# A pause of the attention filled, its second q in two pieces, pooling shared, and the steps ahead of a loop reordered

## The chip, the cores and the metric

The kernel runs on one core of a Trainium2 chip. The metric is the time of one execution on the device in microseconds (us), lower is better. Times stand in the text as the profile gives them: PE is the engine of the matrix products (TensorE), PEld its loads of the stationary operand, DVE is VectorE, ACT is ScalarE, POOL is GpSimd, and SP is SyncE, which here only issues DMAs.

## What is computed

Three stages, in fp32 throughout (cut from the reference):

```python
# attention over pooled keys: q, k, v of shape (8, 8, 576, 64), every 8 rows of k and v averaged
k_p = k.reshape(B, H, 72, 8, D).mean(axis=3)
v_p = v.reshape(B, H, 72, 8, D).mean(axis=3)
attn = softmax(matmul(q, k_p.T) / sqrt(D))
x = matmul(attn, v_p)                       # 4608 rows of 512
# first mixture: rows with x @ w_skip > 0 go through their best of 8 experts
e_idx = argmax(xc @ w_gate); gate_w = softmax(xc @ w_gate)[e_idx]
x[do] = xc + gate_w * (relu(xc @ w1[e]) @ w2[e])
# second stage, for all rows
h = x @ w_in
out = (h / (1 + exp(-h))) @ w_out
```

## The kernel before

**Three stages in time.** The attention takes up to about 147 us, the expert stage from there to about 463 us (a first unit of up to 384 rows until 183 us, the rest in a loop that is entered at 184 us), the dense stage the rest. The change touches the attention's beginning and the step between the first unit and the loop. Every operation is issued through a wrapper that keeps the program's order on its engine (`Ordered`), so all rows of the profile carry line 117, that of its call, and the order in the text of the program is the order in each engine's queue. DMAs on a queue go in the order in which they are issued.

**The attention** (`attention`, line 180) treats 36 tiles of 128 rows, nine for a pair of batches of 576 rows: tiles 0 to 3 are the first 512 rows of batch 0, tiles 4 to 7 those of batch 1, and tile 8 is the last 64 rows of both. Tile 4 is thus the first that needs anything of batch 1. For each tile the steps are: `products` (line 291), eight matmuls of q with the pooled keys in block form (kbd) into PSUM tiles named s; `scores` (line 303), on DVE two maxima (mx) and on ACT eight exponentials (prb); `ptrans` (line 316), five transposes on PE (pt) and two copies on ACT (pts); `pv` (line 326), ten matmuls with the values (vex); and `post` (line 336) on DVE, which begins with sm and divides the row (x). The values of a batch also carry nine columns for routing: `router1` (line 257) transposes the pooled values (vtp, three matmuls), copies them on ACT (vt) and multiplies them with the router's weights wr (cps; the first batch's PSUM tile is named router), and `router2` (line 272) puts the result into vex. A batch is read by SP in three loads: k and v and q, 1152 KB each (`loadk`, `loadv`, `loadq`, lines 203 to 214). `pool_k` (line 216) sums eight rows of k, on DVE as one reduction for each half or quarter of k (kp), on POOL as three adds of halving length; `pool_v` (line 229) does the same for v in five chunks of 128 columns each, as reductions on DVE or adds on POOL; `keys` (line 252) writes kbd on ACT, `values` (line 245) writes vex on POOL.

The start (lines 367 to 388) issues 18 matmuls on a tile of ones (`WARM`, line 54; named warm in the trace), loads half of k0 twice, the constants, q0's first 128 columns, v0 in two pieces, q0's second 128 columns, q0's last 320 columns, wr (72 KB) and k1. The loop over tiles (line 393) runs from -2; its pass i does the scores of tile i+2 up to i = 3 and of i+3 behind it, the transposes of tile i+1, pv and post of tile i. Pass -2 loads v1 and q1 in one piece each, behind k1. DVE pools one half of k1 in pass -1 and the other in pass 0, POOL pools all of v1 in pass -1, and `router1(1)` comes at the end of pass 2. Which pass takes the four quarters of a later batch's k stands in a table (`KEYS`, line 43); that of batch 2 is `(2, 3, 4, 4)`. Batch 2's k and v are issued at the end of pass -2, behind q1.

**The step before the loop** (`first_unit`, line 995, in `moe`, line 852). Products of the unit with w2 of its expert: `mm2_two` (line 938) does sub-tiles 2 and 1, `mm2(0)` (line 926) sub-tile 0, 24 matmuls in eight groups of three (f = 0 to 7), between which steps can be put. Beside them:

- `ffn_ops(0)` (line 1182): four passes of DVE over 128x1024 elements that prepare the dense stage's weights (raw, raw, fr, fr in the trace), all four ahead of `mm2_two`; `ffn_conv3(0)` (line 1198) then casts them on ACT (fh) and subtracts on POOL (fl); `ffn_load(3)` (line 1165) is a load by SP into fr, which can start when fl is done;
- `xtrans` (line 684): transposes of the next unit's gathered rows (xn) on PE (xtp), a cast on ACT (xth) and a subtraction on DVE (xtl), for four chunks of 128 columns, in the order in which the loop's first matmuls (hp) read them;
- two `post` (DVE, x), a scatter (POOL), and small index operations (gi, si).

The loop's first pass then loads the next w1 (SP), does `post(0)`, gathers the rows of the unit after (POOL, xn<-xa), and runs `mm1`: hp (12 matmuls for each of eight f), hh and w2h on ACT. The placing before:

```python
for _ in self.ffn_ops(0):        # all four
    pass
self.rows(gi, nxt)
two = mm2_two()
...
mm2(0, gt, {2: ends, 6: lambda: self.xtrans((2, 3))})
```

Of the kernel before, what the change touches and what calls it, by code (L numbers as in the profile page):

```python
# [5 lines left out]
F32 = mybir.dt.float32  # L6
# [12 lines left out]
P = 128  # L19
# [22 lines left out]
EARLY = 18  # L42
KEYS = {2: (2, 3, 4, 4), 3: (6, 6, 7, 8), 4: (11, 12, 13, 13), 5: (15, 15, 16, 17), 6: (20, 20, 21, 22),
        7: (24, 24, 25, 26)}
# [8 lines left out]
ROWS = WB11, WT[0], WT[1], WB22, WT[2], WB21, WT[3]  # L53
WARM = 18
OPS = [2, 2, 2, 0, 4, 4]
# [104 lines left out]
class Kern:  # L160
# [19 lines left out]
    def attention(self, xa, rs, extra):  # L180
# [3 lines left out]
        with tc.tile_pool(name="as", bufs=1) as s1, \  # L184
# [26 lines left out]

            def loadq(b):
                q_t[b] = s2.tile([P, 4, S], F32, name=f"q{b}", tag="q", bufs=3)
                nc.sync.dma_start(q_t[b], self.qT[b])

            def pool_k(b, eng, halves=(0, 2), n=2):
                k = k_t[b]
                kp = st.get((b, "k"))
                if kp is None:
                    kp = st[b, "k"] = s2.tile([P, 4, G], F32, name=f"kp_{b}", tag="kp")  # L220
                if eng is nc.vector:
                    for a in halves:
                        eng.tensor_reduce(kp[:, a:a + n], k[:, a:a + n], AX.X, ALU.add)
                else:
                    eng.tensor_tensor(k[:, :, :, 0:4], k[:, :, :, 0:4], k[:, :, :, 4:8], ALU.add)
                    eng.tensor_tensor(k[:, :, :, 0:2], k[:, :, :, 0:2], k[:, :, :, 2:4], ALU.add)
                    eng.tensor_tensor(kp, k[:, :, :, 0], k[:, :, :, 1], ALU.add)

# [137 lines left out]
            nc.vector.memset(one, 0.0)  # L366
            self.warm(pp.tile([P, 1024], F32, name="warm", tag="pv"), WARM)
            k_t[0] = s2.tile([P, 4, G, POOL], F32, name="k0", tag="k")
# [3 lines left out]
            nc.scalar.dma_start(self.ident, self.con[:, 0:P])  # L372
            q_t[0] = s2.tile([P, 4, S], F32, name="q0", tag="q", bufs=3)
            nc.sync.dma_start(q_t[0][:, :, 0:P], self.qT[0][:, :, 0:P])
            nc.scalar.activation(one, one, AF.Exp)
            loadv(0)
            nc.sync.dma_start(q_t[0][:, :, P:2 * P], self.qT[0][:, :, P:2 * P])
            nc.sync.dma_start(q_t[0][:, :, 2 * P:S], self.qT[0][:, :, 2 * P:S])
            nc.sync.dma_start(wr, self.wr)
            loadk(1)  # L380
            for i in range(NB):
# [11 lines left out]
            for i in range(-2, NTILE):  # L393
                n = 3 if i > DEEP else 2
                if i > 0 and i + n < NTILE:
                    pss = products(i + n)
                    pts[i + 1] = ptrans(i + 1, prs.pop(i + 1))
                    prs[i + n] = scores(i + n, pss)
                elif i != -1 and i <= DEEP:
                    prs[i + 2] = scores(i + 2)  # L400
                if len(self.to_place) > (3 if i < EARLY else 0) and i < NTILE - 1:
                    self.place(1, nc.scalar.last)
                extra(i, True)
                ready = todo.pop(0) if todo and i < NTILE - 1 else None
                if ready and ready[0]:
                    ready[0]()
                if i == -2:
                    pool_v(0, on_dve=slice(0, 2), rest=slice(2, 3))
                    pool_v(0, on_dve=slice(4, 5), rest=slice(3, 4))
                    values(0)  # L410
                    loadv(1)
                    loadq(1)
                if i == -1:
# [6 lines left out]
                if i == -1:  # L420
                    prs[1] = scores(1, pss)
                    router2(0)
                    pool_k(1, nc.vector, (0,))
                    pool_v(1)
                    values(1)
                if i > 0:
# [20 lines left out]
                if i == 0:  # L447
                    pool_k(1, nc.vector, (2,))
                    keys(1)
                for b in range(B):  # L450
# [4 lines left out]
                    if i + 2 == first[b]:  # L455
                        if b + 2 < B:
                            loadk(b + 2)
                            loadv(b + 2)
                    if i + 2 == first[b] + 3 + (b == 0) and b + 1 < B:
                        router1(b + 1)  # L460
# [391 lines left out]
    def moe(self, xa, up):  # L852
        nc, tc, c = self.nc, self.tc, self.c
        with tc.tile_pool(name="ms", bufs=1) as s1, \
# [140 lines left out]
            def first_unit(cols, nxt):  # L995
                gates()
                nc.vector.tensor_scalar(self.s2, cols[:, U - 1:U], -1.0, None, ALU.add)
                self.ffn_abs(0, self.raw1[:, 0], self.raw1[:, 1])
                for _ in self.ffn_ops(0):
                    pass  # L1000
                self.rows(gi, nxt)
                two = mm2_two()

                def ends():
                    self.xtrans((0, 1))
                    for s in (2, 1):
                        o = self.x4[:, U if s == 2 else s]
                        post(s, two[s], gt, o)
                        if s == 2:
                            scatter(s, o=o)  # L1010
                            nc.vector.tensor_scalar(si[:, 0:U - 1], cols[:, 0:U - 1], -1.0, None, ALU.add)
                    self.ffn_conv3(0)
                    self.ffn_load(3)
                mm2(0, gt, {2: ends, 6: lambda: self.xtrans((2, 3))})

# [967 lines left out]
```

## Time and profile before

| | |
|---|---|
| median of 3 runs | 1229.18 us (1227.0 to 1232.85) |
| the profiled execution | 1231.53 us |
| its span in the profile | 1229.8 us |
| mean granted clock of TensorE | 0.996 of full speed |

All times inside the kernel come from the one profiled execution; its span is 1.73 us shorter than its own time. A timeline's row gives the start and the duration of a run of equal operations in us, the tiles written and read, the shape and their count, and in brackets the idle time of the engine just before with what ended it. "issue" there means that the engine waited for nothing that the profile shows. The clock is granted at one of two levels, 2.4 GHz (1.00 in the rows) or 1.2 GHz (0.50).

### The profile page before, as it was taken

What the parts mean: (1) busy time and instruction counts of PE and PEld (TensorE: products, weight loads), DVE (VectorE), ACT (ScalarE), POOL (GpSimd) and SP (SyncE); (2) the same over time, 40 slices, a digit from 0 to 9 for tenths busy, and PEclk for the clock granted to TensorE, in tenths of its full rate; (3) what the DMA queues carried; (4) which work ended last, traced back from release to release, by engine and by line L of the source; (5) the groups of instructions that cost most, each with busy time, mean ns of one, the idle gap of its engine ahead of it and who ended that gap; (6) DMA issues with size and microseconds to landing.
All of it is one profiled execution on the core that took longest, in us unless ns stands there. A gap on an engine that the chain in (4) does not pass through costs nothing.

```text
span 1229.8 us, 20291 instructions
## 1 busy us (share of the span) xinstructions
PE 1197.8 (97%) x6191; PEld 1014.5 (82%) x6192; DVE 930.5 (76%) x1574; ACT 616.9 (50%) x1290; POOL 395.3 (32%) x347
## 2 busy tenths in 40 slices
PE   8999898999999999999999999999999999999997
PEld 6988788998888888888888888888878888888885
DVE  6888886666776769988678855677897778977767
ACT  6877544445565445454444435554455544555441
POOL 5477532222231220423366823122211221112220
PEclk9999999999999999999999999999999999999999
DMA  9998547565575734558758783677657786575645
GB/s 374 336 305 273 174 138 267 156 213 182 186 252 193 229 139 104 170 165 270 236 180 294 237 248 106 222 202 200 220 187 240 218 232 219 185 245 184 195 159 146
DMA packets 162768, 260.70 MB, mean 212 GB/s; under 512 B 41669, under 2 KB 91461, under 8 KB 160000
## 3 DMA queue, kind: packets, MB, share of 16 engines
q1 hardware_dynamic: 150880, 241.39, 61.2%
q0 software_dynamic: 7008, 16.80, 4.4%
q10 hardware_dynamic: 4800, 1.51, 0.5%
q8 instruction: 42, 0.69, 0.2%
q14 instruction: 38, 0.31, 0.1%
HBM read 203.16 MB, written 59.18 MB: 213 GB/s over the span
## 4 chain that ended last, share of the span: by engine, by line
PE 56%; DVE 2%; DMA 2%; issue 1%; ACT 0%; POOL 0%; POOLq 0%; DVEq 0%
PE ps L117 18%; PE fopy L117 16%; PE fop L117 11%; PE fh L117 11%; DMA wout<-wdo 2%; PE yp L117 1%; PE yz L117 0%; DVE fr L117 0%; DVE accc L117 0%; DVE raw L117 0%; DVE c L117 0%; ACT c L117 0%; DMA out<-oc 0%; DVE w2l L117 0%; PE hp L117 0%
## 5 line engine op out<-in xcount | busy, mean ns | idle before, releaser
L117 PE MATMUL fopy<-c,wout 128*128 128x512 f32 x810 | 192.5, 391 | 1.5 <-DMA wout<-wdo 1.4
L117 PEld LDWEIGHTS fopy<-c,wout 128*128 128x128 f32 x810 | 150.8, 188 | 36.9 <-DVE accc L117 2.6
L117 POOL TENSOR_TENSOR tm<-tm,tm 128x512 f32<-128x512 f32 x24 | 31.8, 1323 | 271.2 <-ACT tm L117 271.2
L117 DVE TENSOR_TENSOR accc<-fopy,accc 128x1024 f32<-128x1024 f32 (+1 forms) x73 | 87.8, 1204 | 22.9 <-PE fopy L117 22.8
L117 ACT ACTIVATE hh<-hp 128x256 fp32r<-128x256 f32 (+1 forms) x96 | 39.5, 411 | 112.1 <-PE hp L117 107.5
L117 DVE TENSOR_TENSOR w2l<-raw,w2h 128x512 fp32r<-128x512 f32 x96 | 65.8, 690 | 27.5 <-ACT w2h L117 20.4
L117 ACT CAST c<-hs 128x512 fp32r<-128x512 f32 x96 | 59.7, 622 | 52.6 <-DVE hs L117 25.9
L117 ACT COPY tm<-ps 128x512 f32<-128x512 f32 x72 | 42.0, 583 | 84.4 <-PE ps L117 84.4
L117 DVE TENSOR_TENSOR c<-hs,c 128x512 fp32r<-128x512 f32 x96 | 66.0, 687 | 23.6 <-ACT c L117 23.6
L117 POOL TENSOR_TENSOR sw<-sw 128x256 f32<-128x256 f32 x64 | 72.4, 1154 | 35.5 <-DVE sw L117 34.2
L117 PE MATMUL fh<-w1l,fh 128*128 128x512 f32 x336 | 83.0, 389 | 0.0
L117 PE MATMUL hp<-xth,w1h 128*128 128x256 f32 (+2 forms) x384 | 72.7, 311 | 7.7 <-issue 3.1
L117 ACT ACTIVATE fsg<-fh 128x512 f32<-128x512 f32 x48 | 28.7, 597 | 91.4 <-PE fh L117 86.9
L117 PEld LDWEIGHTS fh<-w1l,fh 128*128 128x128 f32 x336 | 63.1, 188 | 13.1
L117 POOL DMA_INDIRECT xn<-xa,gi x33 | 38.5, 1165 | 109.4 <-PE hp L117 89.3
L117 PE MATMUL hp<-xth,w1l 128*128 128x256 f32 (+2 forms) x384 | 70.8, 306 | 0.0
L117 PE MATMUL hp<-xtl,w1h 128*128 128x256 f32 (+2 forms) x384 | 70.3, 305 | 0.0
L117 DVE TENSOR_TENSOR fgl<-fsg,fgh 128x512 fp32r<-128x512 f32 x48 | 39.1, 815 | 40.3 <-ACT fgh L117 40.3
L117 PEld LDWEIGHTS hp<-xth,w1h 128*128 128x128 f32 x384 | 59.6, 189 | 12.1 <-issue 6.6
L117 ACT ACTIVATE prb<-s,mx 128x72 f32<-128x72 f32 x288 | 65.4, 355 | 5.8 <-DVE mx L117 5.8
L117 PE MATMUL fop<-fl,fgh 128*128 128x512 f32 x168 | 65.4, 389 | 0.0
L117 PE MATMUL fop<-fh,fgh 128*128 128x512 f32 x168 | 65.4, 389 | 0.0
(260 smaller groups left out, 3025.2 us busy)
## 6 DMA issues: line engine op xcount, KB each, us to landing
raw<-w SPq DMA_DIRECT2D x88, 512.0 KB, 4.8
wout<-wdo SPq DMA_DIRECT2D x135, 256.0 KB
win<-wdi SPq DMA_DIRECT2D x36, 512.0 KB
w1l<-wdi SPq DMA_DIRECT2D x36, 512.0 KB
xa<-x SPq DMA_DIRECT2D x36, 256.0 KB
v<-vR SPq DMA_DIRECT2D x7, 1280.0 KB
w1l<-wdo SPq DMA_DIRECT2D x33, 256.0 KB
fr<-w_in SPq DMA_DIRECT2D x16, 512.0 KB
```

The costliest lines, as they stand in the source:

```text
L117: ins = f(*a, **k)
```

## The change

In the attention: four more matmuls on ones at the start and ten more in pass -2, behind tile 0's scores; wr is issued ahead of q0's last piece; q1 is issued in two pieces, the first 64 columns ahead of v1 and the other 512 behind it. One half of k1 is pooled by POOL in pass -1, ahead of v1; the other stays with DVE in pass 0, and keys(1) is split likewise. Of v1 POOL pools chunks 0 to 2, DVE chunks 3 and 4 in pass 2, behind the maxima of tile 4; values(1) follows there. k2's first quarter moves from pass 2 to pass 3, router1(1) from the end of pass 2 to pass 3, behind scores(5) and ahead of pv(3). In `first_unit`: three of the four operations of `ffn_ops(0)` stay ahead of `mm2_two`; the fourth and gi go behind the transposes of chunks 0 and 1 (still at f = 2); the transposes of chunks 2 and 3 go from f = 6 to f = 4, and the two posts, the scatter, si, the cast and the load go behind them.

```diff
-KEYS = {2: (2, 3, 4, 4), ...
+KEYS = {2: (3, 3, 4, 4), ...
-WARM = 18
+WARM, KEEP = 22, 10
...
-            def loadq(b):
-                q_t[b] = s2.tile([P, 4, S], F32, name=f"q{b}", tag="q", bufs=3)
-                nc.sync.dma_start(q_t[b], self.qT[b])
+            def loadq(b, *parts):
+                if b not in q_t:
+                    q_t[b] = s2.tile([P, 4, S], F32, name=f"q{b}", tag="q", bufs=3)
+                for c in parts or (slice(S),):
+                    nc.sync.dma_start(q_t[b][:, :, c], self.qT[b][:, :, c])
...
                 else:
-                    eng.tensor_tensor(k[:, :, :, 0:4], k[:, :, :, 0:4], k[:, :, :, 4:8], ALU.add)
-                    eng.tensor_tensor(k[:, :, :, 0:2], k[:, :, :, 0:2], k[:, :, :, 2:4], ALU.add)
-                    eng.tensor_tensor(kp, k[:, :, :, 0], k[:, :, :, 1], ALU.add)
+                    for a in halves:
+                        x = k[:, a:a + n]
+                        eng.tensor_tensor(x[:, :, :, 0:4], x[:, :, :, 0:4], x[:, :, :, 4:8], ALU.add)
+                        eng.tensor_tensor(x[:, :, :, 0:2], x[:, :, :, 0:2], x[:, :, :, 2:4], ALU.add)
+                        eng.tensor_tensor(kp[:, a:a + n], x[:, :, :, 0], x[:, :, :, 1], ALU.add)
...
-            nc.sync.dma_start(q_t[0][:, :, 2 * P:S], self.qT[0][:, :, 2 * P:S])
             nc.sync.dma_start(wr, self.wr)
+            loadq(0, slice(2 * P, S))
             loadk(1)
...
+                if i == 2:
+                    pool_v(1, (), slice(3, NC))
+                    values(1)
+                if i == 0:
+                    pool_k(1, nc.vector, (0,))
+                    keys(1, slice(0, 2))
...
                 if i == -2:
+                    self.warm(ones, KEEP)
...
+                    loadq(1, slice(P // 2))
                     loadv(1)
-                    loadq(1)
+                    loadq(1, slice(P // 2, S))
...
-                    pool_k(1, nc.vector, (0,))
-                    pool_v(1)
-                    values(1)
+                    pool_k(1, nc.gpsimd, (2,))
+                    pool_v(1, rest=slice(0, 3))
+                if i == 3:
+                    router1(1)
                 if i > 0:
                     pv(i, pts.pop(i))
...
                 if i == 0:
-                    pool_k(1, nc.vector, (2,))
-                    keys(1)
+                    keys(1, slice(2, 4))
...
-                    if i + 2 == first[b] + 3 + (b == 0) and b + 1 < B:
+                    if i + 2 == first[b] + 3 and 0 < b < B - 1:
                         router1(b + 1)
...
-                for _ in self.ffn_ops(0):
-                    pass
-                self.rows(gi, nxt)
+                ops = self.ffn_ops(0)
+                for _ in range(3):
+                    next(ops)
                 two = mm2_two()
                 def ends():
                     self.xtrans((0, 1))
+                    next(ops)
+                    self.rows(gi, nxt)
+                def sums():
+                    self.xtrans((2, 3))
                     for s in (2, 1):
...
-                mm2(0, gt, {2: ends, 6: lambda: self.xtrans((2, 3))})
+                mm2(0, gt, {2: ends, 4: sums})
```

## Rows read from the trace of the kernel before

**Rows 1.** The page, part 1: busy time, share and instructions of each engine
```profile
PE 1197.8 (97%) x6191; PEld 1014.5 (82%) x6192; DVE 930.5 (76%) x1574; ACT 616.9 (50%) x1290; POOL 395.3 (32%) x347
```

**Rows 2.** Busy time by stretch: stretch, us, PE, PEld, DVE, ACT, POOL, clock, DMA, GB/s
```profile
12.00:15.00 3.00, 3.00 (x15) 2.97 (x15) 1.35 (x3) 0.51 (x2) 2.50 (x7) 0.50 1.09 408
143.00:146.00 3.00, 1.19 (x15) 0.96 (x15) 1.85 (x10) 0.86 (x2) 0.00 (x0) 1.00 0.01 1
213.00:216.00 3.00, 3.00 (x12) 3.00 (x11) 1.45 (x2) 0.46 (x2) 0.23 (x1) 0.51 0.00 0
```

**Rows 3.** Timeline of PE, 0 to 32 us: start us, us, engine, line, operation
```profile
...
1.10 5.90 PE L117 MATMUL warm<-onesb 128*128 128x512 bf16 x18 [1.10 <-DVE one L117]
...
7.58 1.62 PE L117 MATMUL s<-kbd,q 128*128 128x144 f32 x8 [0.58 <-DMA q<-qT]
...
11.60 2.24 PE L117 MATMUL s<-kbd,q 128*128 128x144 f32 x8 [2.40 <-DMA q<-qT]
...
22.78 1.19 PE L117 MATMUL s<-kbd,q 128*128 128x144 f32 x8
...
23.80 1.52 PE L117 MATMUL pt<-ident,prb 128*120 128x128 f32 x5
...
26.87 1.15 PE L117 MATMUL s<-kbd,q 128*128 128x144 f32 x8
...
27.86 0.71 PE L117 MATMUL pt<-ident,prb 128*120 128x128 f32 x5
...
29.80 1.08 PE L117 MATMUL cps<-wr,vt 128*120 128x144 f32 x6
...
```

**Rows 4.** Timelines of POOL and DVE, 9 to 32 us
```profile
...
19.88 4.52 POOL L117 TENSOR_TENSOR v<-v 120x1280 f32<-120x1280 f32 x2 [5.30 <-DMA v<-vR]
...
25.42 0.75 DVE L117 TENSOR_REDUCE kp<-k 128x72 f32<-128x576 f32 x1 [0.25 <-DMA k<-kT]
...
```

**Rows 5.** DMA packets of two stretches: 10 to 11 us, and 16 to 19 us
```profile
...
DMA packets 570, 0.34 MB, mean 339 GB/s; under 512 B 23, under 2 KB 569, under 8 KB 570
...
DMA packets 132, 1.25 MB, mean 416 GB/s; under 512 B 10, under 2 KB 10, under 8 KB 10
...
```

**Rows 6.** Groups by shape up to 45 us (one row); timelines of DVE and ACT
```profile
...
L117 DVE TENSOR_REDUCE vp<-v 120x128 f32<-120x1024 f32 x1 | 1.9, 1882 | 0.0
...
26.76 0.17 DVE L117 TENSOR_SCALAR sm<-pv 128x8 f32<-128x8 f32 x1 [0.59 <-PE pv L117]
...
28.14 0.81 DVE L117 TENSOR_REDUCE mx<-s 128x4 f32<-128x288 f32 x2
...
27.27 0.52 ACT L117 COPY vt<-vtp 64x120 f32<-64x120 f32 x2
...
29.02 1.81 ACT L117 ACTIVATE prb<-s,mx 128x72 f32<-128x72 f32 x8
...
```

**Rows 7.** Timeline of PE, loop's entry, its first pass, start of its second
```profile
...
184.15 1.07 PE L117 MATMUL hp<-xth,w1h 128*128 128x256 f32 x4 [1.04 <-DVE xtl L117]
...
185.06 0.63 PE L117 MATMUL hp<-xtl,w1h 128*128 128x256 f32 x4
...
192.34 0.74 PE L117 MATMUL hp<-xth,w1h 128*128 128x256 f32 x4 [0.52 <-issue]
...
211.88 1.13 PE L117 MATMUL hp<-xth,w1h 128*128 128x384 f32 x4 [2.53 <-issue]
...
```

**Rows 8.** Timelines of DVE, ACT and POOL at the loop's entry
```profile
...
178.90 1.23 DVE L117 SCALAR_TENSOR_TENSOR fr<-raw,fr 128x1024 f32<-128x1024 f32 x1
...
182.43 1.01 DVE L117 TENSOR_TENSOR xtl<-xtp,xth 128x384 fp32r<-128x384 f32 x2
...
191.44 0.38 ACT L117 ACTIVATE hh<-hp 128x256 fp32r<-128x256 f32 x1 [2.88 <-PE hp L117]
...
199.48 3.94 ACT L117 CAST w1h<-raw 128x1024 fp32r<-128x1024 f32 x4
...
187.03 1.03 POOL L117 DMA_INDIRECT xn<-xa,gi  x1 [1.50 <-PE hp L117]
...
```

More of the change, by code (lines that the diff above doesn't have):

```diff
@@ L42 @@
 EARLY = 18
-KEYS = {2: (2, 3, 4, 4), 3: (6, 6, 7, 8), 4: (11, 12, 13, 13), 5: (15, 15, 16, 17), 6: (20, 20, 21, 22),
+KEYS = {2: (3, 3, 4, 4), 3: (6, 6, 7, 8), 4: (11, 12, 13, 13), 5: (15, 15, 16, 17), 6: (20, 20, 21, 22),
         7: (24, 24, 25, 26)}
@@ L366, in attention @@
             nc.vector.memset(one, 0.0)
-            self.warm(pp.tile([P, 1024], F32, name="warm", tag="pv"), WARM)
+            ones = pp.tile([P, 1024], F32, name="warm", tag="pv")
+            self.warm(ones, WARM)
             k_t[0] = s2.tile([P, 4, G, POOL], F32, name="k0", tag="k")
@@ L372, in attention @@
             nc.scalar.dma_start(self.ident, self.con[:, 0:P])
-            q_t[0] = s2.tile([P, 4, S], F32, name="q0", tag="q", bufs=3)
-            nc.sync.dma_start(q_t[0][:, :, 0:P], self.qT[0][:, :, 0:P])
+            loadq(0, slice(P))
             nc.scalar.activation(one, one, AF.Exp)
             loadv(0)
-            nc.sync.dma_start(q_t[0][:, :, P:2 * P], self.qT[0][:, :, P:2 * P])
-            nc.sync.dma_start(q_t[0][:, :, 2 * P:S], self.qT[0][:, :, 2 * P:S])
+            loadq(0, slice(P, 2 * P))
             nc.sync.dma_start(wr, self.wr)
+            loadq(0, slice(2 * P, S))
             loadk(1)
```

## The prediction

> **What bounds the kernel now.** I read the page first: PE is busy for 97% of the span [rows 1], so there is little idle time to win anywhere, and a change of order can win only what PE waits. The granted clock by stretch comes next: the reader sees half clock from 12 to 15 us and again at 213 to 216 us, and full clock in a stretch of 3 us in which PE was busy for only 1.19 us [rows 2]. Then PE's timeline of the beginning: 18 warm matmuls, the scores of tile 0 at 7.58, a pause of 2.40 us until the second piece of q0 lands, and eight score matmuls that take 2.24 us where the same eight later take 1.15 [rows 3]. Further on one place stands out: the transposes of tile 3 take 1.52 us, those of tile 4 take 0.71 [rows 3]. At the loop's entry PE stands still for 1.04 us [rows 7]. These are the places that the change touches. The profiled execution took 1231.53 us, 1.73 more than its span and 2.35 more than the median of 1229.18; the sum below is a difference, made in that execution, and I put it on the median.
>
> **The beginning up to tile 4.** Four more warm matmuls: 18 took 5.90 us, so four cost at most 1.3; PE had 0.58 us idle ahead of tile 0 and 2.40 behind it [rows 3], which covers them: 0. Without that cover, 0.7 us.
>
> KEEP puts ten of the same matmuls into the pause of 2.40: 3.3 us at the mean of those rows, less if the clock is up throughout, so an overrun of 0.9 at most. With no such pause I expect the clock to stay up, and the half clock from 12 to 15 [rows 2] to go. The eight scores alone give back 2.24 - 1.15 = 1.09 us [rows 3]; all of PE's 3 busy us there give back 1.5.
>
> Half (2,) of k1 moves from DVE to POOL. POOL's two big adds of v1 (1280 and 640 elements a partition) took 4.52 us [rows 4], 2.35 ns an element; the three adds of half a k (576, 288, 144) make 2.4 us, those of three chunks of v1 (768, 384, 192) 3.2. POOL had 5.30 us idle before v1 landed [rows 4], which covers the first. wr moves ahead of q0's last piece and makes that 0.2 us later (72 KB at the 416 GB/s of [rows 5]). SP issues one transfer more. All of this lies ahead of tile 4.
>
> Does the 1.5 us get past tile 4? It is the first that reads q1. v1 is there at 19.88, when POOL's wait ends, and k2 at 25.42, when DVE's ends [rows 4]. SP issues q1 between them, and q1 and k2 are equally large (1152 KB), so q1 lands halfway, at 22.65. Tile 4's scores start at 22.78 with no idle time before them [rows 3]: PE and q1 arrive within 0.13 us of each other. The bytes ahead of q1 stay the same. So PE only arrives earlier, at about 21.3, and waits some 1.5 us: **the filled pause is paid back in front of tile 4**, and that wait also covers whatever of the above comes late. What is late next is q1.
>
> The split makes q1 a little later. A piece of 64 columns is 512 runs of 256 bytes. Where q0's short pieces moved, 570 packets went in a microsecond; k1 and v1 went in 132 packets in 3 us, at 416 GB/s [rows 5]. At 570 packets per us the piece takes 0.90 us, against 0.31 for its bytes at 416: the bounds are 0 and +0.6. I take +0.4, nearer the row, whose packets are larger. Tile 4 starts at about 23.05. The Trainium skill, "DMA: Bandwidth & Descriptors", section Specifications, asks for at least 512 bytes for line rate and says that below it the DMA reads, modifies and writes. By that rule the piece could cost twice the upper bound (an estimate), and the sum would be 0.8 us higher; no row here shows such pieces.
>
> **Tile 4 and behind it.** The 0.81 us that tile 3's transposes lost [rows 3] go, since its scores are long done. But DVE gets two chunks of v1 (1.88 us, [rows 6]) right behind tile 4's maxima, ahead of post(2) and of tile 5's maxima, and router1(1) now stands behind scores(5), so ACT's vt copies come after tile 5's eight exponentials. Chain: tile 4's scores 23.05 to 24.2, second maximum to 24.7, chunks to 26.55, post(2) 1.38 from its first instruction to tile 5's maximum [rows 6], so 27.9, first maximum to 28.35, exponentials 1.81 and vt 0.52 [rows 6]: 30.65. The cps matmuls of batch 1 wait for vt; before, they started at 29.80 [rows 3]. So they come 0.85 late, though PE could be there at 29.80 - 0.81 = 29.0. Bounds: -0.8 if DVE and ACT are never late, +1.05 with q1 0.6 late. Neighbours overlap (two maxima of 0.45 take 0.81, [rows 6]), some 0.1 us at each of the chain's steps, so I take **+0.6**. k2's first row moves from tile 2 to tile 3, 0.75 us of DVE [rows 4] ahead of post(3), which pv(4) awaits behind cps and two tiles' scores: 0. values(1) on POOL waits for DVE's chunks until 26.6; its reader is pv(4) too: 0.
>
> **The loop's entry.** PE's idle 1.04 us end with xtl [rows 7]; xtl of chunks 2 and 3 ran from 182.43 to 183.44, behind both posts [rows 8]. Now one ffn operation (1.23, the row at 178.90) goes behind xtl(0, 1), the transposes of chunks 2 and 3 come six matmuls earlier, and both posts and ACT's cast for fh go behind them. DVE: xtl(0, 1) from 178.9 to 179.9, the operation to 181.1, gi, xtl(2, 3) to 182.2. That is 1.2 us before, and ahead of the end of PE's last matmul (184.15 - 1.04 = 183.11, [rows 7]). Queued behind: DVE's work is the same in all, so the posts end where xtl did, 183.4 instead of 182.4, and POOL's scatter and its subtraction for fl come 1.0 later; POOL idled 1.50 us before the loop's gather [rows 8], which covers that. SP's loads of fr and, behind it, of the next w1 wait for fl and are 1.0 later; ACT first reads that w1 at 199.48 [rows 8], 16 us on: 0. Bounds of the gain: at most 1.04 plus the 0.44 that the first four matmuls lost (1.07 against 0.63, [rows 7]); at least 0, since PE stopped again at 192.34 for 0.52 us [rows 7], behind an ACT that had idled 2.88 us until 191.44 [rows 8] on matmuls issued long before. What ends that idle time the rows don't tell; if its end is fixed, PE is caught there as before. I take **-1.04**, the idle time itself.
>
> Sum: 0.6 - 1.04 = -0.44, so 1229.18 - 0.44 = **1228.7 us**. About 0.5%, 6.1 us, is what a measurement of this kernel can tell from no change; this is far inside.
>
> **Rivals.** (a) *q1 is not what tile 4 waits for*, or lands earlier: the 1.5 us carry through, tile 3's 0.81 too, and the entry gives 1.5: 1229.18 - 3.8 = 1225.4. For it: no wait on q1 is named at 22.78. Against it: k2 and v1 leave no earlier place for q1. Chance 0.17.
>
> (b) *The pause moves and the clock falls there; slower.* PE stands before tile 4 for 1.5 to 2 us. Pauses of 2.40 and 2.53 us [rows 3, 7] came with half clock behind them, the stretch with 1.8 us idle in 3 did not [rows 2]; the point that decides lies between. If it falls, 3 us of work at half clock cost 1.5; with 0.6 for the chain and an entry that ACT takes back, 1229.18 + 2.1 = 1231.3. Chance 0.16.
>
> (c) *The short piece costs twice the rate's bound:* 0.8 on the forecast, 1229.5. By [rows 5] it costs less. Chance 0.1. The rule behind it is the Trainium skill's, in the section named above.
>
> (d) *The entry gains nothing*, because ACT's stop ends when it did: 1229.8. For it the row at 192.34 [rows 7]; against it, the stop should follow the loop's start. Chance 0.17. That KEEP fails to hold the clock would change nothing: q1 hides it.
>
> **Numbers.** The forecast has 0.4. The cases reach from 1225.4 to 1231.3; single runs before lie from 1227.0 to 1232.85, so a median of a few can stray by about 1 us that no step explains. Range 1225.0 to 1232.0. No case is 6.1 us away: within 0.5% 0.92, faster by more 0.05 (rival a and a lucky draw), slower by more 0.03.
>
> **What would show it.** Right: full clock from 12 to 15 us; no pause of PE ahead of tile 1's scores; a wait of PE on q of 1.5 us or more that ends near 23; cps of batch 1 near 30.5, behind ACT's vt; at the entry no idle PE ahead of hp. Wrong: tile 4's scores before 22 us (a); half clock between 20 and 28 us (b); POOL's wait for v1 ending after 21 us (c); a stop of PE some 8 us into the loop that is longer than before by what the entry won (d).

## The result, and the profile after

| | before | changed |
|---|---|---|
| median of 8 runs | 1228.22 us (1226.40 to 1232.85) | 1235.68 us (1232.74 to 1237.37) |
| profiled execution, its span | 1231.53, 1229.8 us | 1236.11, 1233.9 us |
| mean granted clock | 0.996 | 0.993 |

The changed kernel is slower: ratio 1.0062, 95% interval [1.0048, 1.0077]. The forecast was 1228.7 within 1225 to 1232, with 0.92 on "within 0.5%". It was wrong, by 7 us and outside its range.

The page's part 1 and a line of its part 3, of the changed kernel (DMA queue, kind: packets, MB, share):

```profile
PE 1201.7 (97%) x6205; PEld 1017.9 (82%) x6206; DVE 937.7 (76%) x1574; ACT 619.0 (50%) x1292; POOL 397.1 (32%) x350
...
q8 instruction: 41, 0.67, 0.2%
```

Against [rows 1] PE has 14 more matmuls, the filling. By its kind the queue q8 brings instructions: 0.67 MB in 41 packets are 16 KB each. (In such lines q1 and q8 are numbers of DMA queues; elsewhere q1 is batch 1's q.) The prediction did not look at these lines; they carry half of the answer.

PE's timeline of the changed kernel, 0 to 36 us, and one row of POOL's:

```profile
1.10 6.63 PE L117 MATMUL warm<-onesb 128*128 128x512 bf16 x22 [1.10 <-DVE one L117]
8.08 1.61 PE L117 MATMUL s<-kbd,q 128*128 128x144 f32 x8 [0.35 <-DMA q<-qT]
9.52 2.32 PE L117 MATMUL warm<-onesb 128*128 128x512 bf16 x10
12.11 1.25 PE L117 MATMUL s<-kbd,q 128*128 128x144 f32 x8 [0.27 <-DMA q<-qT]
...
25.18 2.26 PE L117 MATMUL s<-kbd,q 128*128 128x144 f32 x8 [3.16 <-DMA q<-qT]
27.23 1.27 PE L117 MATMUL pt<-ident,prb 128*120 128x128 f32 x5
...
34.16 1.18 PE L117 MATMUL cps<-wr,vt 128*120 128x144 f32 x6 [0.97 <-ACT vt L117]
...
22.59 2.87 POOL L117 TENSOR_TENSOR v<-v 120x768 f32<-120x768 f32 x2 [2.51 <-DMA v<-vR]
```

The pause of 2.40 us ahead of tile 1 [rows 3] is filled, and tile 1's scores take 1.25 us instead of 2.24. But PE stands for 3.16 us ahead of tile 4, whose scores begin at 25.18 where they began at 22.78, and they and the transposes behind them take up to twice their time. POOL's wait for v1 ends at 22.59, before at 19.88 [rows 4]. Busy time by stretch says why (columns as in [rows 2]):

```profile
12.00:15.00 3.00, 2.84 (x21) 2.43 (x21) 1.82 (x4) 1.29 (x6) 2.84 (x8) 1.00 1.06 415
25.10:28.50 3.40, 3.31 (x14) 3.33 (x15) 1.48 (x3) 0.38 (x1) 2.17 (x5) 0.50 0.97 406
182.00:184.00 2.00, 2.00 (x11) 1.64 (x9) 2.00 (x6) 1.20 (x4) 0.41 (x1) 1.00 0.00 0
199.20:206.00 6.80, 6.09 (x20) 5.23 (x21) 4.38 (x6) 5.04 (x8) 1.98 (x2) 0.50 1.01 386
219.70:223.00 3.30, 3.30 (x13) 3.30 (x12) 0.35 (x1) 0.97 (x2) 2.69 (x3) 0.50 0.42 96
```

The half clock left 12 to 15 us and came back behind the pause of 3.16. At the loop's entry (182 to 184) PE is busy throughout, so the idle 1.04 us of [rows 7] are gone; but half clock stands twice behind it: at 199.2 to 206, in the loop's first pass, where the kernel before ran at 1.00, and at 219.7 to 223, at the start of the second pass, as in [rows 2]. The first pass on PE, DVE and POOL, of the changed kernel:

```profile
183.86 0.77 PE L117 MATMUL hp<-xth,w1h 128*128 128x256 f32 x4
...
198.47 0.33 PE L117 MATMUL xtp<-ident,xn 128*128 128x128 f32 x1 [1.97 <-DMA xn<-xa,gi]
199.91 2.40 PE L117 MATMUL xtp<-ident,xn 128*128 128x128 f32 x10 [1.11 <-DMA xn<-xa,gi]
...
218.46 1.08 PE L117 MATMUL hp<-xth,w1h 128*128 128x384 f32 x4 [3.47 <-DVE x L117]
...
183.95 3.17 DVE L117 TENSOR_SCALAR sq<-table 128x3 int32 x1
187.04 0.74 DVE L117 SCALAR_TENSOR_TENSOR x<-yz,gt,xr 128x512 f32<-128x512 f32 x1
187.86 0.70 DVE L117 COPY xr<-xn 128x1040 f32<-128x1040 f32 x1
...
184.64 2.45 POOL L117 TENSOR_TENSOR fl<-fr,fh 128x1024 fp32r<-128x1024 f32 x1
189.50 1.09 POOL L117 DMA_INDIRECT xn<-xa,gi  x1 [2.41 <-DVE hl L117]
```

PE waits 1.97 and 1.11 us for gathered rows (xn), for which it did not wait before, and the second pass begins at 218.46 instead of 211.88 [rows 7]. POOL's first gather starts 5.64 us behind the loop's first hp; before, 2.88 (187.03 [rows 8] less 184.15 [rows 7]). And DVE runs an index operation `sq` of 3.17 us ahead of `post(0)`, a place where before it had none. The diff does not name sq, and its line stands ahead of the loop in both texts; but in the trace of before this operation (128x3) runs at 463.08, behind the loop. So the order on an engine is not everywhere the order of the text, and it has changed here.

### The profile page after: what moved, and what is told of

Its sections match the earlier page's. It is cut to its first block, busy times and chain, and to the rows that moved or that the text cites. A ratio compares the mean times of both kernels' runs of the same rounds, so it can differ in the third digit from the quotient of the medians.

```text
span 1233.9 us, 20346 instructions
## 1 busy us (share of the span) xinstructions
PE 1201.7 (97%) x6205; PEld 1017.9 (82%) x6206; DVE 937.7 (76%) x1574; ACT 619.0 (50%) x1292; POOL 397.1 (32%) x350
## 4 chain that ended last, share of the span: by engine, by line
PE 57%; DVE 2%; DMA 1%; issue 1%; ACT 0%; POOL 0%; ACTq 0%; POOLq 0%; DVEq 0%
PE ps L117 18%; PE fopy L117 17%; PE fh L117 11%; PE fop L117 11%; DMA wout<-wdo 1%; PE yp L117 1%; PE yz L117 0%; DVE fr L117 0%; DVE accc L117 0%; DVE raw L117 0%; DVE c L117 0%; ACT c L117 0%; DVE w2l L117 0%; PE hp L117 0%; ACTq L117 0%
```

## The experiments

Ratios are to the kernel before, run beside it on the same chip, with a 95% interval. Executions with the attention of before reach its last pv at 141.97 us (e3) to 146.50 (e11), and on one chip 1.2 us apart (e2 and e3). So kernels on different chips are compared by these ratios, and small differences between single profiles are not read.

**Which half costs?** e1: the changed kernel with the entry of before.

```diff
-                ops = self.ffn_ops(0)
-                for _ in range(3):
-                    next(ops)
+                for _ in self.ffn_ops(0):
+                    pass
+                self.rows(gi, nxt)
...
-                mm2(0, gt, {2: ends, 4: sums})
+                mm2(0, gt, {2: ends, 6: lambda: self.xtrans((2, 3))})
```

> The changed attention with the step ahead of the loop as before. Theory 1 (the loss sits at the loop's entry): the changed kernel's trace leaves the attention 1.0 us later than before (pv at 146.44 against 145.30), so about 1 us slower than before, 1229 to 1231, and far from the 1235.7 of the changed kernel. Theory 2 (the loss is the attention's): 1234 or more, as the changed kernel. In both: tile 4's scores start near 25, since q1 lands on its last DMA engine 1.5 us behind the fifteen others; if the 16 KB fetch of PE's instructions that ran on that engine at 20.4 us comes at another time here, q1 lands near 23.5 and the scores start with it.

Measured: 1.0045 [1.0032, 1.0057]. e2: the kernel before with the new entry alone, the same lines the other way round.

> The changed step ahead of the loop with the attention as before. In the changed kernel DVE's index operation sq (128x3) stands ahead of the loop, which it did not before, and takes 3.17 us, until POOL's fl ends. Theory 1 (that wait makes the gather of the next rows 2.5 us late, PE waits 3.1 us for them and runs some us at half clock): PE's idle 1.04 us at the entry go, the first pass loses about 5, so 4 us slower than before, 1231 to 1234; sq lasts over 2 us. Theory 2 (the entry is harmless, the attention is what costs): 1226 to 1228.

Measured: 1.0027 [1.0017, 1.0037]. Both halves lose, some 5.5 and 3.3 us; their sum is 8.8, and together they measured 7.5, the same within the intervals. Two causes were to be found.

**The entry: is it sq?** e3 is e2, and e4 the changed kernel, with the line of sq put behind the loop, where the trace of before has it.

```diff
-            cols = nc.value(self.qi[0:1, 0:1], EMPTY, dve)
-            nc.vector.tensor_scalar(self.sq, self.table[:, bass.ds(cols, U)], -1.0, None, ALU.add)
...
+            cols = nc.value(self.qi[0:1, 0:1], EMPTY, dve)
+            nc.vector.tensor_scalar(self.sq, self.table[:, bass.ds(cols, U)], -1.0, None, ALU.add)
```

> As the run before it, and the line that writes sq stands behind the loop, where the instruction was in the kernel before. Theory 1: the entry's gain stays and the late gather goes, 1226.5 to 1228, some 4 us faster than with sq ahead. Rival (the first pass cannot start earlier than its gathers and weight loads let it; sq is not what makes them late): within 1 us of the run with sq ahead. Second rival (fl and the scatter being later make the gather late by 1 us by themselves): gain of half, 1229 to 1231.

> The whole change with the line that writes sq behind the loop. Theory 1: about 5 us faster than the changed kernel, 1229 to 1231, the sum of what the attention alone and the entry with sq late show. Rival (the loss is the attention's): 1234 or more.

Measured: e3 1.0018 [1.0005, 1.0032], e4 1.0050 [1.0033, 1.0067]. So sq is at most a part: against e2, e3 is 0.6 us faster, and that difference is uncertain by 1.6. What remains shows in e3's DVE, POOL and PE, and, for the end of the same chain, in POOL and DVE of the kernel before (last two rows):

```profile
180.62 0.75 DVE L117 SCALAR_TENSOR_TENSOR x<-yz,gt,xr 128x512 f32<-128x512 f32 x1 [1.08 <-PE hp L117]
181.46 1.70 DVE L117 COPY xr<-xn 128x1040 f32<-128x1040 f32 x1
...
179.10 1.02 POOL L117 DMA_INDIRECT xa<-x,sq  x1 [9.82 <-DVE si L117]
180.14 2.46 POOL L117 TENSOR_TENSOR fl<-fr,fh 128x1024 fp32r<-128x1024 f32 x1
184.10 1.03 POOL L117 DMA_INDIRECT xn<-xa,gi  x1 [1.50 <-PE hp L117]
...
193.24 0.33 PE L117 MATMUL xtp<-ident,xn 128*128 128x128 f32 x1 [1.96 <-DMA xn<-xa,gi]
194.85 1.31 PE L117 MATMUL xtp<-ident,xn 128*128 128x128 f32 x10 [1.28 <-DMA xn<-xa,gi]
...
183.12 2.41 POOL L117 TENSOR_TENSOR fl<-fr,fh 128x1024 fp32r<-128x1024 f32 x1
184.86 1.24 DVE L117 COPY xr<-xn 128x1040 f32<-128x1040 f32 x1
```

fl ends at 182.60 and the gather follows 1.50 us later; before, fl ended at 185.53 and the gather came at 187.03 [rows 8]. The same 1.50 stands in nine traces. It is no slack but the end of a chain: posts, scatter, fl, a copy of xr that ends 0.57 us behind fl in these nine (1.70 us long here, 1.24 before, 0.70 where nothing holds it), then the gather. The gather starts 0.93 or 0.94 us behind the end of that copy in every trace but two (e11 and e15, below). e3's loop begins at 179.36, so its gather comes 4.74 us behind hp, 1.86 later than before; and as PE stops less, it reaches xtp 11.65 us behind hp instead of 12.8 (196.95 less 184.15). It then waits 3.24 us for rows, against 1.04 won at the entry, 2.2 net. That 1.0018 of 1228 is 2.2 as well is in part luck: the interval reaches from 0.6 to 3.9 us, and the sum leaves out the stop ahead of the second pass (4.41 us in e3, 2.53 in [rows 7]).

**Can the chain be shortened?** Both are e3 with fl put ahead of the scatter; e15 also has si right behind gi.

```diff
                 def sums():
                     self.xtrans((2, 3))
+                    self.ffn_conv3(0)
...
-                    self.ffn_conv3(0)
                     self.ffn_load(3)
```

> The attention as before, the changed entry, sq behind the loop, and POOL's fl ahead of the scatter instead of behind it. In the profiles so far the first gather of the loop comes 1.50 us behind the end of fl wherever DVE's copy xr<-xn waits for fl, and PE's transposes wait for that gather. Theory 1 (that chain, posts, scatter, fl, copy, gather, is what gives the entry's gain back): fl ends at least 1 us earlier against PE's first hp, the gather comes 1 to 2 us earlier, PE's wait for xn falls from 3.2 us to under 2; 1 to 2 us faster than with fl behind (1.0018), so 1.0000 to 1.0010. Rival (the gathers' landing is set by the DMA traffic of the w1 loads, not by their issue): the gather's issue is earlier, the landing and the ratio are not.

> The attention as before, the changed entry, sq behind the loop, si written right behind gi, and POOL's fl ahead of the scatter. In the run with fl first (1.0068) DVE's si waited 2.21 us for fl, as sq did 3.17 us in the changed kernel, and the posts and the gather with it. Theory 1 (DVE's small index writes and its copy xr<-xn stand while POOL's fl runs; the gather follows fl by a chain): si takes 0.16 us, the first gather comes 2.5 to 3 us behind PE's first hp (4.7 with fl behind), PE's wait for xn falls under 1.5 us; ratio 0.998 to 1.001, against 1.0018. Rival (the landing is set by the traffic of the loads, not by the issue): gather as early, PE's wait for xn still near 3 us, ratio 1.001 to 1.003.

Measured: 1.0068 [1.0052, 1.0084] and 1.0047 [1.0031, 1.0062], both worse. In e11 si was held by fl, and the posts behind it were late. In e15 it was not, and yet the gather did not come earlier; rows of e11's DVE, e15's POOL and e15's SP:

```profile
183.48 2.21 DVE L117 TENSOR_SCALAR si<-table 128x2 int32<-128x2 f32 x1
```
```profile
179.83 2.44 POOL L117 TENSOR_TENSOR fl<-fr,fh 128x1024 fp32r<-128x1024 f32 x1 [9.38 <-ACT fh L117]
182.43 1.04 POOL L117 DMA_INDIRECT xa<-x,sq  x1 [0.16 <-issue]
189.45 1.25 POOL L117 DMA_INDIRECT xn<-xa,gi  x1 [5.98 <-PE hp L117]
...
182.29 0.37 SPq L117 DMA_DIRECT2D fr<-w_in  x1
182.71 0.51 SPq L117 DMA_DIRECT2D fr<-w_out  x1
```

The end of fl at 182.27 lets SP load 512 KB into fr twice, at the moment of the scatter (182.43); the scatter, which landed in 2.78 us in e3, took 6.28 and landed at 188.71, and the gather came 0.74 us behind that landing. In e11 it is the same: 6.03 us, and the gather 0.74 behind. In all other traces the first of these loads is issued when the scatter has landed, and it lands in 2.78 to 2.80 us. Of the orders tried, scatter ahead of fl is the better one.

**The attention: what of it costs?** e5 is the kernel before once more, for a second profile. e6 is before with the filling alone, e7 e1 without it, e8 e1 with q1 whole behind v1.

```diff
# e6, against before
-WARM = 18
+WARM, KEEP = 22, 10
# e7, against e1
-WARM, KEEP = 22, 10
+WARM, KEEP = 18, 0
# e8, against e1
-                    loadq(1, slice(P // 2))
                     loadv(1)
-                    loadq(1, slice(P // 2, S))
+                    loadq(1)
```

> The kernel before once more, for a second profile of it. The profile read for the prediction was of an execution 4 us above the median, and the two kernels that keep the old attention left the attention at 142.0 and 143.1 us (its last pv) against 145.3. Theory 1 (that execution was an ill one in the attention and a lucky one at the loop, where its PE did not wait for the gathered rows): here the last pv starts at 142 to 143.5, PE waits over 1 us for the gathered rows xn, and the span is 1225 to 1228. Theory 2 (PE waits for xn only with a changed entry): no wait for xn.

> The kernel before with only the four and ten more matmuls on ones. Theory 1 (more instructions of PE bring the 16 KB fetch of its program forward, in all three kernels with the new attention it ran at 19.8 to 20.4 us, with the old one at 28.5 to 29.9; it makes one of 16 DMA engines 1.3 to 1.6 us late, and q1 with it): the fetch near 20 us, q1 near 24.1, tile 4's scores there after a pause of PE of about 2.5 us; 1 to 3 us slower than before. Rival (something else of the new attention moves the fetch): fetch at 27 to 30 us, q1 at 22.6, tile 4 there; time within 1 us of before or a little faster.

> The changed attention without its fourteen more matmuls on ones, the entry as before. Theory 1: the fetch falls back to 26 to 30 us, q1 lands near 23.1 (0.5 behind the old one, the price of the short piece), tile 4's scores start there; PE shows the half clock at 12 to 15 us again; 2 to 4 us faster than the changed attention with them (1233.5). Rival (the loss is in the chain behind tile 4, where DVE's chunks of v1 and the late copy of vt hold PE): within 1 us of 1233.5, whatever the fetch does.

> The changed attention with q1 in one piece behind v1, the entry as before. Theory 1 (the fetch, not the short piece, makes q1 late): v1 lands 0.5 us earlier, q1 near 24.0 instead of 24.5, still 1.3 to 1.6 behind its fifteen other engines; 0 to 1 us faster than 1233.5. Rival (the short rows are what costs, or what shifts the landing on one engine): q1 at 22.6, tile 4 there, 2 to 4 us faster.

Measured: e5 1230.5 us (one run) beside a median of 1230.93; e6 1.0009 [0.9997, 1.0022], e7 1.0001 [0.9990, 1.0013], e8 1.0033 [1.0020, 1.0046]. Without the filling the changed attention costs nothing that can be told, with it 4 to 5.5 us, split or not. e5's profile differs from the first one of the same kernel at the loop: PE waits for gathered rows there, which it did not in the first, and its first pass from hp to hp takes 30.10 us, in the first 27.73.

```profile
197.16 1.31 PE L117 MATMUL xtp<-ident,xn 128*128 128x128 f32 x10 [0.66 <-DMA xn<-xa,gi]
```

Tile 4's scores begin at 23.38 in e7 and at 23.89 to 25.18 in the kernels with the filling. What the filling changes ahead of that shows in the DMA rows of 19.5 to 22 us. The changed kernel:

```profile
q1 hardware_dynamic: 425, 0.91, 95.8%
q8 instruction: 1, 0.02, 2.7%
```

Before, one line stands there:

```profile
q1 hardware_dynamic: 126, 1.05, 100.3%
```

One fetch of 16 KB of instructions, at 20.36 us, took 1.10 us on one of the 16 DMA engines. In the trace of before the first one came at 28.55. A load is cut over 16 engines: the trace keeps 16 landings of each. Of q1's, 15 had come by 23.57 and the last came at 25.05 (before: 22.58 and 22.61). The trace does not name a packet's engine; that the late one is the one with the fetch is inferred from times and counts. Every kernel here with its first fetch at 19.7 to 21.3 us had q1's last landing 1.2 to 1.5 us behind the others, every one with it at 26.5 or later at most 0.12.

**Heat, instructions or bytes?** The filling does two things: it keeps PE's clock up, and it is 14 more instructions with their weights. e10 adds 14 matmuls of 16 columns at the start of e7; the pause ahead of tile 1 stays (2.43 us), and nothing reads their results. e9 and e13 are e1 with a filling in fp32, on 64 columns of stationary operand; each such matmul takes about 1 us and stands as two rows in the trace, which is what is counted here. e14 is e6 with e13's filling, e12 the changed kernel without any.

```diff
# e10, against e7
+            for _ in range(14):
+                nc.tensor.matmul(ones[:, 0:16], self.onesb, self.onesb[:, 0:16], start=True, stop=True)
# e9, against e1 (e13, e14: 5, 2; e12: 18, 0 and the old form)
-WARM, KEEP = 22, 10
+WARM, KEEP = 11, 5
-            self.nc.tensor.matmul(o, self.onesb, bc(self.onesb, 1, 4), start=True, stop=True)
+        w = self.onesb.bitcast(F32)
+            self.nc.tensor.matmul(o, w, bc(w, 1, 8), start=True, stop=True)
```

> The changed attention with the entry as before, its fill made of fp32 matmuls on ones, 11 at the start and 5 in the pause, in place of 22 and 10 in bf16: as long, but 16 instructions where the kernel before has 18. Theory 1 (the count of PE's instructions is what costs, by moving the 16 KB fetches): the first fetch at 26 to 30 us, q1 near 23.2 on all its engines, full clock from 12 to 15 us, the fetch near 194 us back at 200 to 204; within 2 us of before (ratio 0.998 to 1.001). Rival (that PE is early and at full clock is what costs, since it then stands longer in front of q1 and of the gathered rows): fetches as in the kernel before, and still 1.003 to 1.005 of it.

> The changed attention without fill, the entry as before, and behind the 18 matmuls at the start fourteen of 16 columns, some 1 us together: the instructions of the fill without its filling. Theory 1: the first fetch at 20 to 21 us, q1 1.3 to 1.6 late, tile 4 near 24.5, and a fetch near 194 us again; ratio 1.003 to 1.005, as with the fill. Rival (early PE and clock): the fetch moves, and the time stays within 0.1% of the kernel without fill (1.0001).

> The changed kernel without its fourteen more matmuls. If the parts add up: the entry's 1.0027 and nothing from the attention without fill (1.0001), so 1.002 to 1.0035, against 1.0062 with the fill. Theory 1 (fetches) asks for a first fetch at 26 to 29 us. Rival (the entry with sq ahead costs more behind the changed attention): 1.004 or more.

> The changed attention, entry as before, its fill made of 5 and 2 fp32 matmuls on ones (each shows as two rows of 0.44 us at full clock, so 14 rows where the kernel before has 18): pause filled, instructions as few as before. The run with 11 and 5 of them was mis-sized: its start took 11.85 us, and its rows were as many as the bf16 fill's, with the first fetch as early. Theory 1 (the count moves the fetch, the fetch makes q1 late): first fetch at 26 to 30 us, all engines of q1 within 0.2 us near 23.2, tile 4 there; ratio 0.998 to 1.001, as without fill (1.0001). Rival (PE early and at full clock stands longer and is throttled later): fetch as late, ratio still 1.003 to 1.005.

> The kernel before with the same 5 and 2 fp32 matmuls as fill and nothing else. Theory 1: fetch at 28 to 30 us, q1 on time at 22.6, PE stands some 1 us before tile 4, full clock from 12 to 15 us; the gain of the fill is paid back there, ratio 0.999 to 1.000. Rival: the 1.5 us are kept, ratio 0.998 or less. Second rival (early PE costs): 1.001 to 1.003.

Measured: e9 1.0044 [1.0027, 1.0061], e10 1.0032 [1.0017, 1.0047], e12 1.0043 [1.0026, 1.0060], e13 0.9997 [0.9984, 1.0010], e14 0.9985 [0.9973, 0.9996].

e9 tells nothing of the question: its filling was too long (11.85 us), tile 0 began at 12.87, and its first fetch came at 26.53, behind q1 (23.21), and so not as early as e1's, as e13's expectation has it. With e10 and e13 there is a table on the changed attention with the old entry: neither filling nor count 1.0001 (e7), count alone 1.0032 (e10), filling alone 0.9997 (e13), both 1.0045 (e1). The clock's gain cannot be told from nothing there, and **the number of instructions ahead of the load costs**. e13's clock from 12 to 15 us was 1.00, e10's 0.65. On the attention of before the filling shows the same: 1.0009 with the early fetch (e6), 0.9985 without it (e14). Where e14's 1.8 us come from is not shown: its tile 4 begins at 22.83 and its cps at 29.73, as before (22.78 and 29.80), so the filled pause was paid back as forecast, and its interval all but touches 1. e12 shows that the entry loses without the filling too. It lost more than the 1.002 to 1.0035 expected from the parts, but its interval reaches down into that.

**Through the first fetch, or through later ones?** Later fetches move as well, and in several kernels much of the loss showed only in the loop's first pass. e16 and e17 are e13 with 18 matmuls of 16 columns, once in tile 6, behind tile 4, and once at the start. The count is the same.

```diff
# e16, in pv
+                for _ in range(18 if t == 6 else 0):
+                    nc.tensor.matmul(ps[:, 0:16], self.onesb, self.onesb[:, 0:16], start=True, stop=True)
# e17, at the start
+            for _ in range(18):
+                nc.tensor.matmul(ones[:, 0:16], self.onesb, self.onesb[:, 0:16], start=True, stop=True)
```

> The changed attention with the old order at the loop's entry and a short fp32 fill (5 and 2 matmuls), that is the kernel that ran at 0.9997 of before, with 18 matmuls of 16 columns added in the attention's sixth tile, after the scores that wait for q1. Theory A (more matmul instructions move TensorE's first fetch of instructions in front of q1, and tile 4 waits for q1): the count stands behind tile 4, so the first fetch stays at 26 to 30 us, q1's last engine is no more than 0.3 us behind the others, tile 4's scores begin at 23.2 to 23.5, and the time is 0.9997 to 1.001 of before (18 short matmuls are worth at most 0.6 us). Theory B (more instructions cost through the later fetches, in the loop's first pass): the later fetches move as they do with the count at the start, and the time is 1.003 or more, the stretch from the loop's entry to its second pass 1.5 us or more longer than in the kernel without them.

> The same kernel with the same 18 matmuls at the start of the attention instead, in front of the fill. Same count as its partner, another place. Theory A: first fetch at about 20 us, q1's last engine 1.3 to 1.6 us behind the others, tile 4's scores at 24.5 to 25, time 1.003 or more of before. Theory B: as its partner, within 0.1%, whatever tile 4 does.

Measured: e16 1.0007 [0.9995, 1.0019], median 1231.48; e17 1.0022 [1.0009, 1.0035], median 1234.44; twelve runs each on one chip, means 2.25 us apart, uncertain by 1.31. First DMA rows of 19.5 to 22 us, PE's rows of tiles 4 and 5, and the stretch 25.4 to 28.8. Of e16:

```profile
q1 hardware_dynamic: 450, 0.93, 98.7%
...
23.27 1.22 PE L117 MATMUL s<-kbd,q 128*128 128x144 f32 x8 [1.72 <-DMA q<-qT]
26.26 1.14 PE L117 MATMUL s<-kbd,q 128*128 128x144 f32 x8
30.81 1.18 PE L117 MATMUL cps<-wr,vt 128*120 128x144 f32 x6 [1.03 <-ACT vt L117]
...
25.40:28.80 3.40, 3.40 (x28) 3.28 (x27) 3.33 (x8) 2.87 (x12) 0.76 (x2) 1.00 0.98 402
```

Of e17:

```profile
q1 hardware_dynamic: 415, 0.89, 94.1%
q8 instruction: 1, 0.02, 2.7%
...
24.97 1.86 PE L117 MATMUL s<-kbd,q 128*128 128x144 f32 x8 [3.15 <-DMA q<-qT]
29.63 1.14 PE L117 MATMUL s<-kbd,q 128*128 128x144 f32 x8
...
25.40:28.80 3.40, 3.40 (x16) 3.34 (x15) 2.39 (x3) 1.30 (x5) 1.74 (x4) 0.50 0.98 407
```

Put behind tile 4, the same instructions leave the first fetch at 27.41 us, q1 whole at 23.13 and the clock up. Put at the start, the fetch comes at 20.15, q1's last landing 1.45 us behind the others (24.83 against 23.38), tile 4 1.70 later, and behind the longer pause the clock falls: tile 5's scores are 3.37 later (29.63 against 26.26). Of that 2.83 us are left at the start of the last pv of the attention (146.72 and 149.55). The loop's first pass, from hp to hp, takes 27.6 us in both. So these 2.25 us are the first fetch ahead of q1, with the longer pause and the clock behind it: the next fetches at the loop stand alike in both, 13.2 and 13.3 us behind hp. What a later fetch costs where it stands otherwise, the pair does not test. e17's ratio came out under the 1.003 expected, e16's inside its bounds.

## Why the prediction was wrong

**The filled pause** went as worked out: no pause ahead of tile 1, full clock at 12 to 15 us, eight scores in 1.25 us, and all of it paid back in front of tile 4, by a wait for q1.

**"The bytes ahead of q1 stay the same" is the step that failed first.** It looked at data. The instructions count too: the term for them was missing, and it measured 1.5 us on q1 (the last landing at 25.05, the others by 23.57). With it goes the zero for the warm matmuls, "which covers them: 0": the idle time covered their durations, not what their number does to the time of the fetch. That time is not a matter of plain counting: PE had some 135 matmul rows behind it at the first fetch of the kernel before, and 93 in e6, 14 of them the added ones. What sets it stays open. The split itself was sized right: +0.4 forecast, and without a fetch q1's last piece was whole at 23.20 in e13 against 22.70 in e14, where q1 is in one piece, +0.5; e1 and e8, which differ in the split alone, show the same on the 15 landings (23.14 and 22.61). Twice the rate's bound (rival c) did not come; its mark did, POOL's wait for v1 past 21 us, but by the fetch: 15 of v1's landings had come by 20.93, the last came at 22.52.

The Trainium skill, "Runtime: NRT & Kernel Launch", section Instruction fetch mechanics, says that an engine's instructions are brought in blocks of 16 KiB by a DMA queue of its own and that this is mostly hidden. The size agrees (0.67 MB in 41 packets). Hidden it is for PE, which shows no idle time at the fetch of the kernel before (28.55 us), but not for the loads under way, whose last landings come 1.2 to 1.6 us late. The measurement decides.

**Rival b, the clock that falls behind the pause,** came true at 25.1 to 28.5 us. It was given 0.16 since the pause was put at 1.5 to 2 us; it was 3.16. A pause of that size does not decide alone: e1 (3.04) and e4 (3.15) had no half clock behind it, e17 (3.15) and the changed kernel had. Why, these runs leave open.

**Behind tile 4** the chain was right: forecast 30.65 for cps with tile 4 at 23.05, 7.60 us apart; in e16 30.81 and 23.27, 7.54 apart. In the changed kernel half clock stretches it to 8.98. Whether the +0.6 that was put on it is right, 1.0001 of e7 does not tell: cps comes 1.02 us later there than in e5 (30.91 and 29.89), on the same chip, and the interval is as wide.

**The entry: "POOL idled 1.50 us before the loop's gather, which covers that" failed.** The gain at hp came as forecast (no idle PE at 183.86), though the 1.04 were those of one execution: in e5 the stop is 0.69. The posts, scatter and fl were later, as forecast (fl by 1.52 us, where 1.0 was forecast). But the 1.50 were the tail of the chain that leads to the gather, and the row named PE's hp as its releaser, which misled: an idle time that is the same 1.50 in kernel after kernel is a latency, not a reserve. The forecast of -1.04 became +3.3 (e2), +2.2 with sq out of the way (e3). How much later the gather could come shows at a row of PE's timeline of the kernel before that the prediction did not read:

```profile
196.95 1.47 PE L117 MATMUL xtp<-ident,xn 128*128 128x128 f32 x12
```

PE did not wait there, but the last of the three gathers had landed only at 196.81: the reserve was 0.14 us, in e5 there was none, and the new order asked for 1.86 of the gather and 1.15 of PE. Behind those waits the clock fell in the changed kernel (199.2 to 206), in e3 it did not. Rival d's stop is there as well (0.87 ahead of hp at 189.14 in the changed kernel), but it is not what cost.

**sq was not foreseen.** It came to stand ahead of `post(0)` once the steps around it had moved, and there it met POOL's work: 3.17 us for an operation on three columns, where gi, of the same shape, takes 0.16. The Trainium skill, "SBUF — State Buffer", section SBUF: two separate sides, says that GpSimd and a DVE operation in a two-port mode, or with two inputs in SBUF, share a pair of ports as an exclusive lock, which the one that starts first holds for its whole instruction while the other is blocked. The trace agrees where fl had started first: si ran until fl's end in e11 (2.21), and the copy of xr took 1.70 instead of 0.70 in e3. sq too ended with fl (187.12 and 187.09), but it began 0.69 us ahead of it, beside the scatter; what held it until then, and in which mode these operations run, no trace here tells. Its price in the total is not settled: 0.6 us by e2 and e3, uncertain by 1.6.

**What stays open.** The count costs 0.15% in the one pair on one chip, 0.31% and 0.48% where e10 and e1 are held against kernels on other chips. The part above 0.15% shows in the loop's first pass in some profiles and not in e16 and e17; it is not explained. One rival is left: in e1, e4, e6, e8 and the changed kernel, whose first pass takes 32.5 to 34.6 us, a fetch comes 11 to 13 us behind hp, while the gathered rows are under way. But it does so in e10 too (11.3), whose pass takes 30.1, as e5's does without any change. For the entry, e2 shows that it loses; that the late gather is why rests on the traces, since neither attempt to bring the gather forward did so.

## What to carry to other kernels

Filler matmuls are not free where PE is idle: here 14 to 18 more of them moved the first fetch of instructions 6 to 9 us forward, and a fetch that met a load made the load's last landing 1.2 to 1.6 us late. Look in the DMA rows for an instruction packet beside the load that is waited for. Filling with few long instructions rather than many short ones avoided it: seven filler matmuls in fp32, five in place of the 18 in bf16 and two in the pause, measured 0.9985 [0.9973, 0.9996] of the kernel before (e14), a small gain whose place is not shown. Before an idle time is taken as cover, ask whether it has the same length wherever it stands; if it has, it is the tail of a chain, and what moves its head moves its end.

## What the runs showed of the hardware that was not expected

- A fetch of 16 KB of instructions took 0.9 to 2.2 us in these traces (1.10 in the changed kernel's first), and the loads around it had one of their 16 landings late for three transfers in a row (v1 1.59, q1 1.48, k2 1.48 us in the changed kernel), by more than the fetch itself took.
- An fp32 matmul stands as two rows in the trace (5 and 2 of them gave 10 and 4 rows), so counts of rows are not counts of the program's calls. The eight matmuls of a tile's scores are four calls of `products`; the five transposes of a tile are five rows.
- The releaser that a row names can differ where the order is the same: with the old entry PE's stop ahead of the loop is put down to xtl in [rows 7] (1.04 us) and in e5 (0.69), and to ACT's xr in e16 (1.25) and e17 (1.26).
